# A planned attention-and-MLP kernel whose order planner gets other landing latencies for software loads, and an order searched with them

## The chip, the cores and the metric

The kernel runs on one core of one Trainium2 chip. Its engines are TensorE (PE in the profile, with its weight loads as PEld), VectorE (DVE), ScalarE (ACT), GpSimd (POOL) and SyncE (SP). The metric is the device time of one execution in microseconds, lower is better; it is given as the median of several runs. One execution is also recorded by the hardware profiler.

## The reference

Two stages follow each other. The first is causal attention in a window of 128 positions with ALiBi slopes, over 8 batches and 8 heads, 576 positions and a head dimension of 64. The second is a two-layer MLP with a squared ReLU over the 4608 tokens.

```python
scores = scale * q @ k.T                      # per batch and head, 576 x 576
mask = (rel >= 0) & (rel < 128)               # rel = query position - key position
scores = where(mask, scores - slope[h] * abs(rel), -1e9)
attn = exp(scores - max); attn /= sum(attn)
x = (attn @ v) laid out as 4608 tokens x 512
h = x @ w_in                                  # 512 x 2048
out = (relu(h) ** 2) @ w_out                  # 2048 x 512, float32
```

## The kernel before, in words

**Tiles.** The 576 positions of a batch are five blocks: four of 128 and one of 64. There are 40 blocks (m = 0 to 39), numbered in the order in which they are handled: first block 0 of every batch (m = 0 to 7, "diag": only the block's own keys), then the others, two batches at a time. The 4608 tokens are nine groups g of 512 tokens, each of four ranges of 128 tokens; a range is one block, or two half blocks. A block's path is: load of k, q and v (cast to bf16 by the load), transposes of k and q (`tp`, on PE for m below 8, by a DMA transpose issued on SP after that), scores (`s`, L520), exp (`e`, ACT), mask (`m`, DVE), product with v (`pv`, L587), reciprocal and norm (`r`, `n`, DVE), transpose of x into `xT` (`xp`, on PE for m below 8, a DMA transpose on SP after that, L617).

**MLP steps.** For groups 0, 1 and 2 the first product is done in small units: `u{g}.{r}.{e}` (L721) multiplies range r of the group (128 tokens in group 0, 256 in groups 1 and 2) with 4 or 2 column blocks of `w_in`, so that one unit always fills a PSUM bank of 512 columns. Later groups use `fc{g}.{fc}` (L739) on 512 tokens. Each is followed by a relu on ACT (L692) and a square on DVE (L683). The second product is `o{g}.{t}.{part}` (L766), a quarter of the contraction over 2048 for 128 tokens: four matmuls of 512 columns. The work list puts all first-product steps of group 0 first, and then alternates one first-product step of group g+1 with one output step of group g. Item i has key 4i.

**Weights.** `w_in` and `w_out` are loaded in four quarters each (i0 to i3 and o0 to o3, L357 and L360) by software loads issued on POOL, as are all blocks but k and q of block 0, which come by hardware queues of SP and ACT. In group 0 a unit of element e needs quarter ie of `w_in`. `FIRST` is the order in which POOL issues the blocks 0 to 7 and the eight quarters.

**The planner.** `Plan` does not run on the chip: it fixes, when the kernel is built, the order in which every engine gets its instructions. Each task has an engine or a choice of them, a duration, a key and what it depends on. `Plan.order` steps through time by its own model: among the tasks that an engine could start within `NEAR` ns of the earliest, it takes the one of lowest key. A transfer takes the DMA engines from `max(start + FIRST, dma_free)` for `dma` ns, and counts as landed `LAND` ns (or the task's own `lat`) after that:

```python
at = max(st + self.FIRST[e], self.dma_free)
self.dma_free = at + t.dma
t.end = self.dma_free + (self.LAND[e] if t.lat is None else t.lat)
```

At most eight transfers of each kind (software or hardware) are outstanding (`LANES`). What an engine gets is then executed in order: when the plan believes that a load lands earlier than it does, the instruction that needs it stands in the queue, and everything behind it on that engine waits too. Where the plan sees PE idle for over 200 ns in its first 30 us, `fill` puts small matmuls on zeros into the gap (L269), in number 0.7 of the gap divided by 56 ns. `ADJ` adds an amount to the key of single named tasks; it is the result of a search. Blocks from 8 on have the key of the first work item that needs them, less `LEAD`. `N_CUT` blocks have their `xT` copied in two halves, and the first `N_PVH` jobs take the PSUM banks of `pv` from ring "h" (two banks, shared with the units and transposes) instead of ring "a" (four banks, shared with the scores).

Of the kernel before, what the change touches and what calls it, by code (L numbers as in the profile page):

```python
# [9 lines left out]
BF16 = mybir.dt.bfloat16  # L10
# [2 lines left out]

FIRST = ["b0", "b1", "b2", "i0", "i1", "o0", "i2", "b3", "i3", "o1", "o2", "o3", "b4", "b5", "b6", "b7"]
DIAG = [[0], [1], [2], [3], [4, 5], [6, 7]]
N_HW = 1
N_PE = 8
N_CUT = 2  # L20
N_PVH = 1
N_WARM = 8
FILL = 0.7
LEAD = 1160
IOTA = 3
TP, XP = "h", "h"
UNITS = {0: 128, 1: 256, 2: 256}
CUT = 384
SIZE = {"kq": 4, "v": 9, "kqT": 7, "P": 3, "x": 3}
DUE = {m: 200.0 * m - 1e5 for m in range(40)}  # L30

ADJ = {
    "e1.1": 9000135.6, "e19.2": -177.01, "e19.3": -468.76, "e2.1": 100084.3, "m2.0": 690.7, "m6.1": 98674.82,
    "mask0.6": 99479.82, "n6.1": 98853.62, "o0.1.2": -273.16, "o0.2.1": 39, "o0.3.2": -120.75, "o1.1.0": -108.3,
    "o1.2.3": -99095.7, "o1.3.1": -36.0, "o1.3.2": -98248.6, "o1.3.3": -224.85, "o2.0.0": -99746.7, "o2.0.1": -614.83,
    "o2.0.2": -99764.0, "o2.0.3": -321.48, "o2.2.1": -99007.0, "o2.3.0": -99983.4, "o2.3.1": -875.31,
    "pv0.1": 99179.79, "pv17.0": -148.06, "r0.1": 582.3, "reluu0.0.1": -99432.0, "reluu0.2.2": -9000091.1,
    "reluu0.2.3": -99589.6, "reluu1.0.0": -99692.3, "reluu2.1.2": -52.84, "s13": 168.43, "s17": -99446.52,
    "s20": 342.83, "squ0.1.0": 48, "squ0.2.3": 99864.0, "u0.1.0": -79.4, "u0.1.1": -99420.7, "u0.2.1": -99696.3,
    "u0.2.3": -98883.7, "u1.0.1": -98012.9, "u1.1.3": -99531.7, "u1.1.5": 191.7, "u1.1.6": -410.31,  # L40
    "u2.0.4": -100055.4, "u2.0.5": -342.1, "u2.0.6": -100078.7, "u2.0.7": -331.83, "u2.1.1": 78.7, "u2.1.2": 63.7,
    "u2.1.3": -99113.3, "u2.1.4": -79.4, "u2.1.7": -303.48,
}


def FUSED(g, u):
    return False


class Task:  # L50
# [20 lines left out]
class Plan:  # L71
# [2 lines left out]
    LAT = {"PE": 210.0, "ACT": 60.0, "DVE": 80.0, "POOL": 200.0, "SP": 200.0, "ACTQ": 200.0}  # L74
    BEGIN = {"POOL": 840.0, "SP": 740.0, "ACTQ": 740.0, "ACT": 2550.0, "DVE": 860.0, "PE": 1190.0}
    FIRST = {"POOL": 1100.0, "SP": 1150.0, "ACTQ": 1150.0}
    LAND = {"POOL": 1200.0, "SP": 2200.0, "ACTQ": 900.0}
    TO_SP = 600.0
    LANES = 8
    NEAR = {"PE": 60, "ACT": 0, "DVE": 25}  # L80
    FILL_UNTIL = 30000.0

    def __init__(self, bufs):
# [108 lines left out]
def kernel(  # L192
    ctx: ExitStack, tc: tile.TileContext, q, k, v, moe_w_in, moe_w_out, out
):
    nc = tc.nc
# [78 lines left out]
    def act(n):  # L274
        return n * 0.95 + 115.0
# [4 lines left out]
    def dve_p(n, rate=1):  # L280
        return n / rate / 0.96 + 185.0
# [65 lines left out]
    t_zero = plan.add({"DVE": 1300.0}, -1e5 + 950, zero, name="zero", later=25000.0)  # L347


    t_win = [None] * 4  # L350
    t_wout = [None] * 4

    def load_w(which, n, key):
        def emit():
            w = d_ff // 4
            if which == "in":
                nc.gpsimd.dma_start(w_in_sb[:, :, n * w:(n + 1) * w],  # L357
                                    moe_w_in[:, n * w:(n + 1) * w].rearrange("(c p) f -> p c f", p=128))
            else:
                nc.gpsimd.dma_start(w_out_sb[:, 4 * n:4 * n + 4, :],  # L360
                                    moe_w_out[n * w:(n + 1) * w, :].rearrange("(c p) f -> p c f", p=128))
        t = plan.add({"POOL": 780.0}, key, emit, dma=2600.0, name=f"w_{which}{n}")
        (t_win if which == "in" else t_wout)[n] = t

    s_kq, s_v, t_kq, t_v = {}, {}, {}, {}

# [7 lines left out]
    def load_block(m, key):  # L374
# [10 lines left out]
        if split:  # L385
            stage = stages[m]
            t_l = []
            for i, src in enumerate((k, q)):
                for r, (eng, e) in enumerate((("SP", nc.sync), ("ACTQ", nc.scalar))):
                    def fetch(i=i, src=src, r=r, e=e):  # L390
                        e.dma_start(view(stage, i)[:, r], source(src, m, split)[:, :, r])
                    t_l.append(plan.add({eng: 740.0}, key + 0.1 * i, fetch, dma=330.0, lat=1000.0,
                                        name=f"l{'kq'[i]}{m}.{r}"))

            def cast_kq(i):
                w = slice(i * d_model, (i + 1) * d_model)
                copy((c_k, c_q)[i],
                     kq[s_kq[m].idx][:, w].rearrange("s (i r d) -> s r i d", i=4, d=D),
                     stage[:, w].rearrange("s (r i d) -> s r i d", r=2, d=D))
            engs = {"DVE": 480.0, "ACT": 600.0} if m else {"DVE": 480.0}  # L400
            c_q = None
            c_k = plan.add(engs, key, lambda: cast_kq(0), t_l[0:2], [s_kq[m]], name=f"ck{m}")
            c_q = plan.add(engs, key, lambda: cast_kq(1), t_l[2:4] + [c_k], name=f"cq{m}")
            t_kq[m] = [c_k, c_q]
        else:
            def fetch_kq():
                for i, src in enumerate((k, q)):
                    nc.gpsimd.dma_start(view(kq[s_kq[m].idx], i), source(src, m, split))  # L408
            t_kq[m] = [plan.add({"POOL": 1780.0}, key, fetch_kq, [], [s_kq[m]], dma=2 * ns,
                                name=f"lkq{m}", count=2)]  # L410
# [229 lines left out]


    def ups(g):
        if UP[g] == 512:
            return [("fc", g, u) for u in range(16)]
        return [("unit", g, r, e) for r in range(512 // UP[g]) for e in range(16 * UP[g] // 512)]

    UP = {g: UNITS.get(g, 512) for g in range(NG)}
    work_list = ups(0)
    for g in range(NG):
        up = ups(g + 1) if g + 1 < NG else []  # L650
# [1 line left out]
            work_list += up[u:u + 1] + [("o", g, u // 4, u % 4)]  # L652

    def span_of(item):
        w = UP[item[1]]
        lo = item[1] * 512 + (item[2] * w if w < 512 else 0)
        return lo, lo + w

    def blocks(lo, hi):
        return [at[x] for r in range(lo // 128, hi // 128) for x in ranges[r]]  # L660
# [10 lines left out]

    g_slots, g_sq, g_first, o_slots = {}, {}, {}, {}

    def relu_square(g, slot, last_mm, key, out_of, fused):
        def square(a, b=None):
            if g_slots[g].tile is None:
                g_slots[g].tile = work.tile([128, FCB, 512], BF16, tag="g", bufs=2, name="g")
            o = out_of(g_slots[g].tile)
            i = a if len(o.shape) == 2 else a.rearrange("p (f t) -> p f t", f=o.shape[1])
            if fused:  # L680
                nc.vector.scalar_tensor_tensor(o, i, 0.0, i, op0=ALU.max, op1=ALU.mult)
            else:
                nc.vector.tensor_tensor(o, i, i, op=ALU.mult)  # L683
        if fused:
            ts = plan.add({"DVE": dve_p(512)}, key, lambda: square(slot.tile), [last_mm] + g_sq[g][:1], [], [slot],
                          name=f"rs{g}")
        else:
            srt = Slot("rt")

            def relu():  # L690
                srt.tile = work.tile([128, 512], BF16, tag="rt", bufs=3, name="rt")
                nc.scalar.activation(srt.tile, slot.tile, AF.Relu, bias=0.0, scale=1.0)  # L692
            tr = plan.add({"ACT": act(512)}, key, relu, [last_mm], [srt], [slot], name=f"relu{last_mm.name}")
            ts = plan.add({"DVE": dve(512, 2)}, key, lambda: square(srt.tile), [tr] + g_sq[g][:1], [], [srt],
                          name=f"sq{last_mm.name}")
        g_sq[g].append(ts)
        return ts

    def group(g):
        if g not in g_slots:  # L700
# [1 line left out]
            return [g_slots[g]]  # L702
        return []

    sq_of = {}

    def unit(g, r, e, key):

        new = group(g)
        slot = Slot("h")  # L710
        w = UP[g]
        nf = 512 // w
        lo = g * 512 + r * w
        ms = blocks(lo, lo + w)

        def emit():
            fill(t_mm, bank_of(slot, "h"))
            for f in range(nf):
                fc = nf * e + f
                for cc in range(C):  # L720
                    nc.tensor.matmul(slot.tile[:, f * w:(f + 1) * w], w_in_sb[:, cc, fc * 128:(fc + 1) * 128],  # L721
                                     xT[:, cc, lo:lo + w], start=cc == 0, stop=cc == C - 1)
        t_mm = plan.add({"PE": 4 * nf * mm(w)}, key, emit,
                        [t_win[nf * e // 4], g_first.get(g)] + [x for m in ms for x in t_x[m]], [slot] + new,
                        name=f"u{g}.{r}.{e}")
        g_first.setdefault(g, t_mm)
        ts = relu_square(g, slot, t_mm, key,
                         lambda gt: gt[:, nf * e:nf * e + nf, r * w:(r + 1) * w], FUSED(g, e + r))
        for t in range(r * w // 128, (r + 1) * w // 128):
            sq_of.setdefault((g, t, nf * e // 4), []).append(ts)  # L730

    def fc_step(g, fc, key):
# [3 lines left out]
        def emit():  # L736
            bank(slot, "h")
            for cc in range(C):
                nc.tensor.matmul(slot.tile, w_in_sb[:, cc, fc * 128:(fc + 1) * 128],  # L739
                                 xT[:, cc, g * 512:(g + 1) * 512], start=cc == 0, stop=cc == C - 1)  # L740
        t = plan.add({"PE": 4 * mm(512)}, key, emit,
                     [t_win[fc // 4], g_first.get(g)] + [x for m in blocks(g * 512, g * 512 + 512) for x in t_x[m]],
                     [slot] + new, name=f"fc{g}.{fc}")
        g_first.setdefault(g, t)
        ts = relu_square(g, slot, t, key, lambda gt: gt[:, fc, :], FUSED(g, fc))
        for r in range(4):
            sq_of.setdefault((g, r, fc // 4), []).append(ts)

# [84 lines left out]
```

The softmax here doesn't subtract the row's maximum and nothing guards it: scores larger than these inputs give would overflow.

## Time and profile before

| What | Value |
|---|---|
| runs | 316.77 us, median of 3 (316.46 to 316.91) |
| profiled execution | 316.23 us, its span 314.4 us |
| mean granted TensorE clock | 0.994 |
| software loads (queue 0) | 18.10 MB |
| weight quarters, issue to landing | w_in 10.9 us, w_out 15.0 us (medians of 4) |
| block loads, issue to landing | 6.2 to 7.6 us (medians) |

The span runs from the first to the last instruction; the time has 1.8 us more around it. A digit of a slice row is the busy share of 1/40 of the span in tenths, and the row PEclk is the clock granted to TensorE. In a group's row, busy time and mean duration are followed by the idle time ahead of it and by what ended it. A matmul's duration includes its way through the array, so matmuls in a row overlap; how many start in a stretch says more than their mean duration.

### The profile page before, as it was taken

To read this page: it belongs to the slowest core of one execution; us is meant where nothing else is said; L and a number is where in the kernel's file an instruction comes from. 1 tells how busy PE (TensorE), PEld (TensorE's weight loads), DVE (VectorE), ACT (ScalarE), POOL (GpSimd) and SP (SyncE) were. 2 spreads that over 40 slices of the span, in tenths; PEclk is the share of its full clock that TensorE was granted. 3 is DMA by queue.
4 is the path that set the end of the run, shared out by engine and by line. 5 is a ranking of instruction groups with operands and counts; after the bars stand their busy time and mean duration, and the time that the engine had idled before them with its cause. 6 is when DMAs were issued, how large, how long until landed. Compare 5 with 4: busy or idle time off the path is not lost.

```text
span 314.4 us, 7113 instructions
## 1 busy us (share of the span) xinstructions
PE 306.3 (97%) x2794; PEld 176.0 (56%) x2794; DVE 174.1 (55%) x498; ACT 170.7 (54%) x331; POOL 105.5 (34%) x131
## 2 busy tenths in 40 slices
PE   8789999999999999999999999999999999999996
PEld 4679756776766755454554555545554444444443
DVE  3756467766566666776766666666666222222211
ACT  4646436657657625776576655576464443434400
POOL 8826598352622666320966301800000000000000
PEclk9979999999999999999999999999999999999999
DMA  9999999999999999994999999992221100010022
GB/s 134 181 190 206 171 184 163 160 153 171 187 138 138 162 189 167 181 143 95 127 196 170 180 107 122 191 161 83 52 63 23 67 35 34 34 35 33 33 93 76
DMA packets 165714, 39.54 MB, mean 126 GB/s; under 512 B 156336, under 2 KB 161200, under 8 KB 165680
## 3 DMA queue, kind: packets, MB, share of 16 engines
q0 software_dynamic: 114656, 18.10, 84.5%
q1 hardware_dynamic: 50592, 20.65, 34.9%
q8 instruction: 22, 0.36, 0.5%
q10 hardware_dynamic: 432, 0.33, 0.3%
q14 instruction: 12, 0.10, 0.1%
HBM read 36.70 MB, written 9.44 MB: 147 GB/s over the span
## 4 chain that ended last, share of the span: by engine, by line
PE 92%; DMA 5%; POOL 2%; issue 0%; ACT 0%; POOLq 0%
PE o L766 39%; PE h L739 27%; PE h L721 14%; PE pv L587 6%; PE s L520 5%; DMA w_in_sb<-in_moe_w_in_dram 3%; DMA xT<-x 2%; POOL kq L408 1%; POOL vf L413 1%; PE tp L464 1%; PE xp L629 0%; POOL w_in_sb L357 0%; POOL dist L304 0%; ACT osb L290 0%; POOLq L304 0%
## 5 line engine op out<-in xcount | busy, mean ns | idle before, releaser
L766 PE MATMUL o<-w_out_sb,g 128*128 128x512 bf16 (+2 forms) x592 | 142.4, 373 | 0.0
L692 ACT ACTIVATE rt<-h 128x512 bf16<-128x512 f32 x144 | 85.8, 609 | 91.4 <-PE h L739 63.3
L683 DVE TENSOR_TENSOR g<-rt 128x512 bf16<-128x512 bf16 x144 | 60.3, 422 | 66.8 <-ACT rt L692 66.0
L739 PE MATMUL h<-xT,w_in_sb 128*128 128x512 bf16 x384 | 96.1, 379 | 0.0
L766 PEld LDWEIGHTS <-g 128*128 128x128 bf16 x592 | 54.5, 98 | 56.5
L544 ACT ACTIVATE P<-s 128x512 bf16<-128x512 f32 (+1 forms) x136 | 67.2, 582 | 17.3 <-PE s L520 17.3
L739 PEld LDWEIGHTS <-w_in_sb 128*128 128x128 bf16 x384 | 34.6, 98 | 38.2
L552 DVE TENSOR_TENSOR P<-P,masks 128x512 bf16<-128x512 bf16 (+1 forms) x112 | 44.6, 405 | 14.7 <-ACT P L544 9.8
L721 PE MATMUL h<-xT,w_in_sb 128*128 128x128 bf16 (+1 forms) x512 | 47.9, 250 | 3.0 <-DMA w_in_sb<-in_moe_w_in_dram 2.3
L408 POOL DMA_DIRECT2D kq<-in_k_dram x39 | 33.4, 856 | 36.4 <-DMA kqT<-kq 26.9
L721 PEld LDWEIGHTS <-w_in_sb 128*128 128x128 bf16 x512 | 39.7, 100 | 8.7 <-DMA w_in_sb<-in_moe_w_in_dram 2.7
L413 POOL DMA_DIRECT2D vt<-in_v_dram x32 | 27.2, 855 | 46.2 <-PE pv L587 43.7
L408 POOL DMA_DIRECT2D kq<-in_q_dram x39 | 33.5, 860 | 8.3 <-DMA kq<-in_q_dram 2.4
L609 DVE TENSOR_TENSOR x<-pv,rec 128x256 bf16<-128x256 f32 (+1 forms) x80 | 33.8, 423 | 2.7
L587 PEld LDWEIGHTS <-P 128*128 128x128 bf16 (+1 forms) x576 | 25.6, 101 | 14.1 <-DVE P L559 1.7
L290 ACT ACTIVATE osb<-o 128x512 f32<-128x512 f32 (+1 forms) x24 | 14.2, 590 | 23.4 <-PE o L766 23.4
L605 DVE RECIPROCAL rec<-pv 128x4 f32<-128x4 f32 (+1 forms) x80 | 14.2, 178 | 22.7 <-PE pv L587 20.2
L587 PE MATMUL pv<-vt,P 128*128 128x65 bf16 (+1 forms) x448 | 24.0, 194 | 0.0
L288 DVE COPY osb<-o 128x512 f32<-128x512 f32 (+1 forms) x13 | 8.9, 681 | 15.1 <-PE o L766 14.6
L520 PEld LDWEIGHTS <-kqT 64*128 64x128 bf16 x448 | 12.4, 94 | 7.6 <-issue 7.2
L520 PE MATMUL s<-kqT 64*128 64x128 bf16 (+1 forms) x256 | 15.6, 210 | 0.0
L520 PE MATMUL s<-kqT,kqT 64*128 64x128 bf16 (+1 forms) x192 | 11.4, 210 | 0.0
(40 smaller groups left out, 96.3 us busy)
## 6 DMA issues: line engine op xcount, KB each, us to landing
out_dram<-osb SPq DMA_DIRECT2D x31, 256.0 KB, 5.1
kq<-in_k_dram POOLq DMA_DIRECT2D x31, 128.0 KB, 6.9
kq<-in_q_dram POOLq DMA_DIRECT2D x31, 128.0 KB, 7.6
vt<-in_v_dram POOLq DMA_DIRECT2D x24, 128.0 KB, 7.6
w_in_sb<-in_moe_w_in_dram POOLq DMA_DIRECT2D x4, 512.0 KB, 10.9
w_out_sb<-in_moe_w_out_dram POOLq DMA_DIRECT2D x4, 512.0 KB, 15.0
vf<-in_v_dram POOLq DMA_DIRECT2D x8, 128.0 KB, 6.2
out_dram<-osb SPq DMA_DIRECT2D x8, 128.0 KB, 2.4
```

Source lines behind the costliest of these rows:

```text
L408: nc.gpsimd.dma_start(view(kq[s_kq[m].idx], i), source(src, m, split))
L413: nc.gpsimd.dma_start(tile_of(s_v[m])[0:n, :, 0:D], source(v, m))
L520: nc.tensor.matmul(sS[2 * g2 + r].tile[:, jj * 256 + c0:jj * 256 + c0 + w], tile_of(s_kqT[mk])[rows, c, :], tile_of(s_kqT[mq])[rows, C + c ...
L544: nc.scalar.activation(flat(Pt[sP.idx]), sS[i].tile.rearrange("p (j t) -> p j t", j=2)[:, :, lo:hi], AF.Exp, bias=0.0, scale=scale)
L552: nc.vector.tensor_tensor(flat(Pt[sP.idx]), flat(Pt[sP.idx]), flat(masks), op=ALU.mult)
L587: nc.tensor.matmul(sv.tile[0:n, hi * (D + 1):(hi + 1) * (D + 1)], Pt[sP.idx][:, place(h)].rearrange("p t q -> p (t q)")[:, w], tile_of(s_v ...
L609: nc.vector.tensor_tensor(xt[sx.idx][0:n, hf * 256:(hf + 1) * 256].rearrange("p (h e) -> p h e", h=4), heads(sv)[0:n, :, 0:D], sr.tile[0:n ...
L683: nc.vector.tensor_tensor(o, i, i, op=ALU.mult)
L692: nc.scalar.activation(srt.tile, slot.tile, AF.Relu, bias=0.0, scale=1.0)
L721: nc.tensor.matmul(slot.tile[:, f * w:(f + 1) * w], w_in_sb[:, cc, fc * 128:(fc + 1) * 128], xT[:, cc, lo:lo + w], start=cc == 0, stop=cc ...
L739: nc.tensor.matmul(slot.tile, w_in_sb[:, cc, fc * 128:(fc + 1) * 128], xT[:, cc, g * 512:(g + 1) * 512], start=cc == 0, stop=cc == C - 1)
L766: nc.tensor.matmul(slot.tile[:, 0:hi - lo], gt[:, fc, t * 128:(t + 1) * 128], w_out_sb[:, fc, lo:hi], start=fc == 0, stop=fc == FCB - 1)
```

## The change

The latency from the end of a software transfer to its landing becomes 2400 ns for blocks (1200 before) and 2900 ns for weights. The two k loads of block 0 get 1650 ns and the two q loads 700 ns (1000 before). In `FIRST` block 3 moves ahead of the third quarter of `w_in`. `N_CUT`, `N_PVH`, `LEAD` and `NEAR` get other values, and `ADJ` is another table. The unit sizes are written as lists with the same sizes as before, the quarters of `w_in` as a list `PIECES` of four equal pieces, and a path for a fused relu and square that was never taken is removed.

```diff
-FIRST = ["b0", "b1", "b2", "i0", "i1", "o0", "i2", "b3", "i3", "o1", "o2", "o3", "b4", "b5", "b6", "b7"]
+FIRST = ["b0", "b1", "b2", "i0", "i1", "o0", "b3", "i2", "i3", "o1", "o2", "o3", "b4", "b5", "b6", "b7"]
...
-N_CUT = 2
-N_PVH = 1
+N_CUT = 1
+N_PVH = 0
...
-LEAD = 1160
+LEAD = 720
...
-UNITS = {0: 128, 1: 256, 2: 256}
+UNITS = {0: [(0, 128, 4), (128, 128, 4), (256, 128, 4), (384, 128, 4)], 1: [(0, 256, 2), (256, 256, 2)],
+         2: [(0, 256, 2), (256, 256, 2)]}
+PIECES = [4, 4, 4, 4]
...
 ADJ = {
...
-    "u2.1.3": -99113.3, "u2.1.4": -79.4, "u2.1.7": -303.48,
+    "e1.2": 99737.5, "e14.1": 197.91, "e16.2": -128.81, "e19.2": -8999803.95, "e2.3": -401.4, "e20.1": 2.03,
+    "e3.1": 99809.35, "e6.3": 99108.3, "fc3.1": -547.61, "fc3.2": -237.14, "fc3.3": -684.14, "fc3.5": -652.43,
+    "fc3.7": -100007.3, "fc3.8": -9000379.3, "m18.2": 165.47, "m18.3": -239.22, "n1.1": 100203.0, "n10.1": 495.17,
...
+    "u0.2.0": -8999828.5, "u0.2.1": -99868.0, "u1.1.0": 39, "u1.1.1": -99305.4, "u1.1.4": -99991.3,
...
 }
...
-    LAND = {"POOL": 1200.0, "SP": 2200.0, "ACTQ": 900.0}
+    LAND = {"POOL": 2400.0, "SP": 2200.0, "ACTQ": 900.0}
...
-    NEAR = {"PE": 60, "ACT": 0, "DVE": 25}
+    NEAR = {"PE": 25, "ACT": 60, "DVE": 25}
...
-        t = plan.add({"POOL": 780.0}, key, emit, dma=2600.0, name=f"w_{which}{n}")
+        t = plan.add({"POOL": 780.0}, key, emit, dma=650.0 * (hi - lo), lat=2900.0, name=f"w_{which}{n}")
...
-                    t_l.append(plan.add({eng: 740.0}, key + 0.1 * i, fetch, dma=330.0, lat=1000.0,
+                    t_l.append(plan.add({eng: 740.0}, key + 0.1 * i, fetch, dma=330.0, lat=700.0 if i else 1650.0,
...
-            tr = plan.add({"ACT": act(512)}, key, relu, [last_mm], [srt], [slot], name=f"relu{last_mm.name}")
+        tr = plan.add({"ACT": act(n)}, key, relu, [last_mm], [srt], [slot], name=f"relu{last_mm.name}")
...
-        ts = relu_square(g, slot, t_mm, key,
-                         lambda gt: gt[:, nf * e:nf * e + nf, r * w:(r + 1) * w], FUSED(g, e + r))
+        ts = relu_square(g, slot, t_mm, key, lambda gt: gt[:, nf * e:nf * e + nf, at_r:at_r + w], nf * w)
```

In every unit `nf * w` is 512, so relu and square keep their shapes.

## The prediction

> **What bounds the kernel now.** I read the page first. Its engine shares and its 40 slices say that TensorE is the bound, and that it is short of full at the two ends only.
>
> ```profile
> span 314.4 us, 7113 instructions
> PE 306.3 (97%) x2794; PEld 176.0 (56%) x2794; DVE 174.1 (55%) x498; ACT 170.7 (54%) x331; POOL 105.5 (34%) x131
> PE   8789999999999999999999999999999999999996
> PEclk9979999999999999999999999999999999999999
> ```
>
> The third digit of PEclk is a 7: the clock fell once, between 15.7 and 23.6 us. "Busy" hides that, so I cut this stretch out with the table by stage (columns: us, then busy us and instructions of PE, PEld, DVE, ACT, POOL, then granted clock, DMA share, GB/s).
>
> ```profile
> 14.00:17.56 3.56, 1.24 (x20) 1.01 (x18) 1.75 (x7) 0.98 (x2) 0.85 (x2) 0.95 1.24 207
> 17.56:20.80 3.24, 3.24 (x36) 3.24 (x37) 1.02 (x4) 0.60 (x1) 1.20 (x2) 0.53 1.26 203
> 20.80:25.69 4.89, 4.89 (x80) 4.42 (x78) 2.80 (x18) 3.98 (x12) 2.47 (x4) 1.00 1.84 182
> ```
>
> TensorE is idle for 2.3 of the first 3.56 us and then runs at 0.53 of its clock for 3.24 us (0.47 x 3.24 = 1.5 us lost). Together 3.8 us of TensorE time go here. The PE timeline names the waits.
>
> ```profile
> 14.99 1.07 PE L721 MATMUL h<-xT,w_in_sb 128*128 128x128 bf16 x16 [0.93 <-DMA w_in_sb<-in_moe_w_in_dram]
> 15.89 0.28 PE L629 MATMUL xp<-ident,x 128*128 128x128 bf16 x2
> 17.56 1.89 PE L721 MATMUL h<-xT,w_in_sb 128*128 128x128 bf16 x16 [1.40 <-DMA w_in_sb<-in_moe_w_in_dram]
> 19.25 0.64 PE L587 MATMUL pv<-vf,P 128*128 128x65 bf16 x8
> ```
>
> The first quarter of w_in (i0) lands at 14.99, the second (i1) at 17.56. An i1 unit stands in PE's in-order queue ahead of block 2's pv, whose last mask ended at 16.70 on DVE, and ahead of every further i0 unit. From 17.56 on TensorE never waits for more than 0.65 us until the tail. So the end moves only by what is saved near the start, unless a later supply runs out.
>
> **The change part by part.**
>
> *Landing constants.* I follow the planner's transfer clock by hand. The stage loads of block 0 and its v end at 4080, kq1 at 5820, v1 6690, kq2 8430, v2 9300, i0 11900, i1 14500, o0 17100 ns. With LAND 1200 it believes kq1 at 7.0, kq2 at 9.6, i0 at 13.1, i1 at 15.7, o0 at 18.3 us. With 2400 for blocks and 2900 for weights it believes 8.2, 10.8, 14.8, 17.4, 20.0. The trace: PE waits for q1 until 8.16, q2 until 10.77, i0 until 14.99, i1 until 17.56; POOL's last w_out issue waits for o0 until 20.34. The new beliefs are right to about 0.3 us, the old ones 1.1 to 2.0 early. A rule speaks against two constants: the Trainium skill, "DMA: Bandwidth & Descriptors", section "Anatomy of one DMA — SWDGE (gpsimd) path", gives a software load a fixed part of about 2.0 us that scales with nothing. With it i0 would be expected at 13.9 and the plan would still place things 1.1 us early. The landings leave 2.3 us for q2 (10.77 - 8.43) and 3.1 for i0 (14.99 - 11.90), so I take the change's values.
>
> *What that can fill.* Between 14.99 and 17.56 the work with i0 alone is the units of rows 0, 1 and 2 (0.89 us each, the chain's row "27.16 0.89 PE h L721 x16"), pv2 (two bursts of 0.24) and xp2 (0.22): 2.67 + 0.70 = 3.4 us for 2.57 us of time. Row 2 is the late one: s2 ran at 12.0, its exps end at 13.5, masks and norms are short on DVE, so x2 can be there near 16.7. ADJ's entry for "u0.2.0" (-8999828.5) asks for just that unit early. So this stretch can be full, and then no half clock follows. Waits that the planner now foresees also get fill matmuls (line 269), which the before lacks at 14 to 17.6 because it foresaw none.
>
> *b3 ahead of i2.* Three block loads of 0.87 us of issue each pass one weight issue on POOL and one transfer on the software queue. In the before i2 landed by 23.15 (POOL's wait ends there) and i3 by 28.24; b3's three transfers lie between and take 28.2 - 23.1 - 2.6 = 2.5 us. So i2 comes 2.5 us later, near 25.6; b3 comes 2.6 us earlier: k, q, v near 20.9, 21.7 and 22.5. i3 and everything behind it keep their places: POOL's eight outstanding loads only swap whom they wait for, and the order behind i3 is the same. SP and ACT issue nothing of this.
>
> *The sum at 25.6 us.* In the before, 7 units and 1 output step had begun and ended there (timeline to 25.69): 7 x 0.89 + 0.86 = 7.1 us, beside pv2 and xp2. In the changed order what exists before i2 is 6 units (rows 0 to 2 with i0 and i1), 3 output steps with o0 (20.3 us on), and b3's tp, s and pv: 5.34 + 2.58 + about 1.15 (tp 0.45, s 0.45, pv 0.25) = 9.1 us. It fits: i1 units from 17.6 to 20.3, output steps to 22.9, b3 between, then a hole of about 1.7 us until i2, unavoidable as nothing else has landed. Gain 9.1 - 7.1 = 2.0 us, and behind it both orders are full. Its ends: 3.4 us if i2 and b3 land as the planner believes (25.2) and the hole holds more of b3; 1.0 if the queue is blocked again by a landing that is 0.3 to 0.5 us late.
>
> *Clock at that hole.* A rule is to be weighed here. The row: the stretch 14.00 to 17.56 held 1.24 us of work, its longest gap was 1.40 us, and the half clock followed. The Trainium skill, "TensorE: Matmul & The Clock Gate", section "HAM oscillation — how this bites in real kernels", asks only that no idle gap exceed about 3.4 us; by it neither this drop nor one at the new hole should occur, and the 1.5 us would be no part of any sum. The row decides: a stretch 35% busy was enough. The new hole leaves its stretch about half busy, more with fills; the stretch 12.00 to 14.00 in the before was 74% busy and kept the clock. Cost between 0 and 1.5 us; I take 0, being nearer to the stretch that kept it once fills run.
>
> *N_CUT 1, N_PVH 0.* One xT copy for block 1 instead of two of 0.38 us on ACT: 0.2 us saved on an engine that waits for PE then; the whole x1 now waits for the second norm (DVE 0.42), hidden by i0's landing at 14.99. Block 0's pv takes "a" banks, which can hold back s1 by a norm (0.6 us) at 9.4 us; five microseconds of cover remain before i0. Both zero; with the cover gone 0.2 and 0.6.
>
> *LEAD 720, NEAR, ADJ.* The last group's blocks get due 960 - 720 = 240, the key of work item 60, which PE has passed by about 85 us; all other blocks stay at or near the front as before. So LEAD should move little by itself. The stall of 0.65 us at 80.52 (PE waits for a transposed block) is a misplaced wait: six output steps of group 1 were still undone. A new order may drop it or put another in its place: 0.65 either way, I take +0.3.
>
> Units keep their sizes, w_in its four pieces, relu and square their 512 columns (ACT 609, DVE 422 ns): zero, as the instructions are the same.
>
> Sum: 2.0 + 0.3 = 2.3 us off the profiled execution (316.23; span 314.4 and 1.8 around it), which is 0.5 under the median of the runs. Off the median: **316.77 - 2.3 = 314.5**.
>
> **The rivals.**
>
> *The gain is given back later.* Blocks come at DMA's pace, and being ahead uses up slack. From the chain I counted output steps: when group 1's first unit starts at 51.2 one step of group 0 is left; at 80.52 six steps of group 1; at 120.5, when group 3 starts, one step of group 2.
>
> ```profile
> 51.37 1.75 PE h L721 x16
> 74.45 6.03 DMA xT<-x
> 80.52 2.79 PE h L721 x24
> 117.42 1.73 PE o L766 x8
> 119.70 0.97 PE o L766 x4
> 120.67 1.73 PE h L739 x8
> ```
>
> Group 3 needs block 16's transpose, issued on SP at 111.81, plus the page's 5.7 us to landing: 117.5. At 117.5 four output steps (3.5 us) were left. So up to about 3.5 us of gain survives there. If half of that slack is not usable in queue order, 1 us survives: 315.8.
>
> *Half clock at the new hole.* 2.0 + 0.3 - 1.5 to 1.7 = 0.6 to 0.8 off: about 316.1. For it: 35% busy was enough. Against: fills.
>
> *Slower: block 16 comes a turn later.* The 32 transposes of x run from 63.7 to 242.0 us, one per 5.75 us. If the altered keys let another block's SP transpose pair go first, block 16 lands near 123.3 instead of 117.5. PE, 2.3 us ahead, has 3.5 - 2.3 = 1.2 us left at 117.5 and stands idle 4.6 us: net 2.3 us slower, 319.1. It decides from a delay of 3.5 us on (there the early gain is eaten up). Against it: SP's order follows block order, and PE waits in the before are small.
>
> *The change doesn't do what it says:* the other order is as good as the old and the landings only move a wait from i1 to i2: within 0.6 us of the before, 316.6.
>
> **How the numbers follow.** This kernel's measurement tells about 0.2% (0.63 us) from no change. The early hole filled, gain 1.2 to 3.4: 0.68. Given back later, gain 0.7 to 1.2: 0.09. Half clock at the hole: 0.10, of which 0.06 count as faster. No effect: 0.05. Slower: 0.08. So faster 0.83, same 0.09, slower 0.08. The range 313.3 to 316.4 runs from a gain of 3.4 to the half-clock case and leaves out the slow case and half of "no effect".
>
> **What would show it.** In the changed profile: three i0 units and pv2 before the first i1 unit; granted clock near 1 from 15 to 21 us; b3's tp at 21 to 22 instead of 25.7; a hole or line-269 fills just before 25.6; group 1's first unit about 2 us before 51.2 and group 3's about 2 us before 120.5; the tail (last 16 us) unchanged. I am wrong if the clock falls again near 25 to 28, or if PE idle appears at 51, 80 or 118.

## The result, and the profile after

The changed kernel takes 314.24 us (median of 4 runs, 313.98 to 314.68), the kernel before 316.76 (median of 4). The ratio is 0.9923 with a 95% interval of 0.9906 to 0.9940: 2.5 us, or 0.8%, faster. The profiled executions stand closer, 316.23 and 314.68 (spans 314.4 and 312.9): that of the kernel before is below all its other runs, that of the changed kernel is its slowest. What follows explains the 1.5 us between these two, and uses ratios for what is beyond them.

The changed kernel's page, and its table by stage for the stretches shown of the kernel before (us, then busy us and instructions of PE, PEld, DVE, ACT, POOL, then granted clock, DMA share, GB/s):

```profile
span 312.9 us, 7112 instructions
PE 302.9 (97%) x2777; PEld 175.3 (56%) x2820; DVE 171.1 (55%) x492; ACT 173.2 (55%) x336; POOL 105.6 (34%) x131
```

```profile
14.00:17.56 3.56, 2.43 (x42) 2.07 (x41) 1.96 (x9) 1.86 (x5) 0.80 (x2) 1.00 1.24 207
17.56:20.80 3.24, 2.67 (x38) 2.36 (x40) 2.71 (x9) 1.91 (x7) 1.04 (x2) 1.00 2.07 169
20.80:25.60 4.80, 4.80 (x71) 3.89 (x70) 2.52 (x17) 2.42 (x8) 3.09 (x4) 1.00 1.31 205
```

The clock stays at 1.00 (0.53 before in the second row), and PE has 2.43 us of work instead of 1.24 in the first. The matmul counts are not to be compared closely: records are missing here (2777 matmuls beside 2820 weight loads), so some of the "idle" of PE is none. The PE timeline shows what the order has become:

```profile
15.18 1.07 PE L718 MATMUL h<-xT,w_in_sb 128*128 128x128 bf16 x16 [0.94 <-DMA w_in_sb<-in_moe_w_in_dram]
16.20 0.41 PE L593 MATMUL pv<-vf,P 128*128 128x65 bf16 x8
16.61 0.39 PE L635 MATMUL xp<-ident,x 128*128 128x128 bf16 x4
17.76 1.96 PE L718 MATMUL h<-xT,w_in_sb 128*128 128x128 bf16 x32 [0.39 <-DMA w_in_sb<-in_moe_w_in_dram]
...
50.22 1.91 PE L718 MATMUL h<-xT,w_in_sb 128*128 128x256 bf16 x16
...
78.13 1.91 PE L718 MATMUL h<-xT,w_in_sb 128*128 128x256 bf16 x16
...
118.60 3.62 PE L735 MATMUL h<-xT,w_in_sb 128*128 128x512 bf16 x16
```

Block 2's pv stands ahead of the first i1 unit. The first unit of group 1 starts at 50.22, the first of group 2 at 78.13. In the kernel before they start at 51.20 and at 80.52, the second after a wait of 0.65 us:

```profile
51.20 1.91 PE L721 MATMUL h<-xT,w_in_sb 128*128 128x256 bf16 x16
80.52 2.79 PE L721 MATMUL h<-xT,w_in_sb 128*128 128x256 bf16 x24 [0.65 <-DMA xT<-x]
```

The waits of PE in the changed kernel (us in total, times, longest) hold no more than 0.4 us behind 25 us:

```profile
PE s L526 <- DMA kqT<-kq: 0.2, 1, 0.2
PE o L762 <- issue: 0.2, 1, 0.2
```

So the gain is 1.0 us by 50 us and 2.4 us at group 2's start, of which 1.5 are left at the end. Of the 2.4 us, 1.0 is the early part, 0.65 the wait that is gone, and the rest is work that is still to be done. The table by stage for the output steps alone (L766 before, L762 after; PE, then weight loads) counts them up to group 2's start, first before, then changed:

```profile
0.00:80.50 80.50, 25.72 (x104) 9.27 (x104) 0.98 1.80 169
```

```profile
0.00:78.10 78.10, 23.16 (x90) 8.95 (x100) 1.00 1.81 169
```

Four weight loads are one step: 26 steps before, 25 after, while units (384 weight loads), scores (128) and pv (112) are the same. One step is 0.86 us, and 2.39 - 0.86 = 1.53 us.

**Where the other wait went.** The timeline of SP, first of the kernel before, then of the changed one:

```profile
63.72 1.20 SPq L617 DMA_TRANSPOSE xT<-x  x1
73.12 1.23 SPq L450 DMA_TRANSPOSE kqT<-kq  x1
74.45 1.29 SPq L617 DMA_TRANSPOSE xT<-x  x1
```

```profile
67.52 2.51 SPq L623 DMA_TRANSPOSE xT<-x  x2
72.32 7.45 SPq L456 DMA_TRANSPOSE kqT<-kq  x3
```

Block 9's x is complete when its last norm ends at 70.06 us on DVE in the kernel before. Its transpose is issued only at 74.45, because block 12's kq transpose stands ahead of it in SP's in-order queue and waits for its load (SP's waits there: "SPq L450 <- DMA kq<-in_k_dram: 7.5, 1, 7.5"). The old plan starts that transpose at about 67.8 us (the edit of experiment 5 puts block 9 just ahead of it), 5 us before it could be issued. In the changed kernel x of blocks 8 and 9 go first, at 67.5, and block 12's transpose follows at 72.3. Group 2's first unit needs blocks 8 and 9.

### The profile page after: what moved, and what is told of

Its sections match the earlier page's. It is cut to its first block, busy times and chain, and to the rows that moved or that the text cites. A ratio compares the mean times of both kernels' runs of the same rounds, so it can differ in the third digit from the quotient of the medians.

```text
span 312.9 us, 7112 instructions
## 1 busy us (share of the span) xinstructions
PE 302.9 (97%) x2777; PEld 175.3 (56%) x2820; DVE 171.1 (55%) x492; ACT 173.2 (55%) x336; POOL 105.6 (34%) x131
## 4 chain that ended last, share of the span: by engine, by line
PE 78%; DMA 16%; POOL 3%; issue 1%; ACT 0%; POOLq 0%; SPq 0%
PE o L762 34%; PE h L735 27%; PE h L718 7%; PE pv L593 5%; PE s L526 5%; DMA w_out_sb<-in_moe_w_out_dram 5%; DMA kqT<-kq 3%; DMA vf<-in_v_dram 3%; DMA kq<-in_q_dram 3%; DMA w_in_sb<-in_moe_w_in_dram 2%; POOL kq L414 2%; POOL vf L419 1%; POOL vt L419 0%; POOL dist L305 0%; ACT osb L291 0%
## 5 line engine op out<-in xcount | busy, mean ns | idle before, releaser
L762 PE MATMUL o<-w_out_sb,g 128*128 128x512 bf16 (+2 forms) x565 | 138.4, 373 | 1.9 <-DMA w_out_sb<-in_moe_w_out_dram 0.3
L735 PE MATMUL h<-xT,w_in_sb 128*128 128x512 bf16 x368 | 95.1, 379 | 0.8
L762 PEld LDWEIGHTS <-g 128*128 128x128 bf16 x592 | 54.1, 98 | 56.0 <-issue 0.4
L718 PE MATMUL h<-xT,w_in_sb 128*128 128x128 bf16 (+1 forms) x512 | 46.7, 246 | 1.3 <-DMA w_in_sb<-in_moe_w_in_dram 1.3
L291 ACT ACTIVATE osb<-o 128x512 f32<-128x512 f32 (+1 forms) x23 | 13.6, 592 | 21.0 <-PE o L762 20.8
```

The lines of the kernel that those rows point to most:

```text
L762: nc.tensor.matmul(slot.tile[:, 0:hi - lo], gt[:, fc, t * 128:(t + 1) * 128], w_out_sb[:, fc, lo:hi], start=fc == 0, stop=fc == FCB - 1)
```

## The experiments

Kernel n below is the kernel of experiment n. Beside these kernels the runs of the kernel before lie between 315.6 and 319.8 us (median 316.8 to 316.9 in each of three sets), so each kernel is given as a ratio to it with its interval, beside what its profile shows. Moves of single instructions are made by changing the planned start of a task after `plan.order()` and sorting again.

**1. Fills at the two early waits of the kernel before.**

```diff
+            for _ in range({"u0.0.0": 12, "u0.1.1": 20}.get(t_mm.name, 0)):
+                nc.tensor.matmul(slot.tile[:, 0:128], warm[:, 0:128], warm[:, 0:128], start=True, stop=True)
```

> The kernel before with 12 matmuls on zeros put ahead of the first i0 unit and 20 ahead of the first i1 unit, into PE's waits of 0.93 and 1.40 us; no other instruction moves. If the half clock from 17.6 to 20.8 us is what the idle of that stretch costs, the clock stays at 1.00 and the time falls by its loss of 1.5 us: about 315.3. If the half clock has another cause (the rival), or if the gain of the change is idle time filled with useful work alone, the time stays within 0.3 us of the kernel before.

Measured: 0.9914 (0.9881 to 0.9947), about 2.7 us (2.1 us between the medians); clock 1.00, and a mean clock of 0.999 or 1.000 in all six executions. But its profiled execution is only 0.8 us shorter than that of the kernel before (span 313.6), and that 0.8 us is seen at group 2's start: 79.69 instead of 80.52, with a wait of 0.74 us for block 9. What PE gained early beyond that stood still there. The time agrees with the first theory, the profile doesn't show the path; the two are not reconciled. Block 12's kq transpose was issued at 72.45 there, 0.7 us earlier than in the kernel before; whether loads came earlier still in the other executions is not on record.

**2. Block 2's pv ahead of the first i1 unit in the kernel before** (`"u0.1.1": 17325.0`).

> The kernel before with one unit, u0.1.1 (the first that needs i1), moved behind the two pv bursts of block 2 in PE's order; all else as it was. If the wrong landing cost 0.5 us of useful work stuck behind the i1 wait and no more, the time falls by 0.5 us: 316.3. If the 0.5 us of work are also enough to keep the clock (busy share of the stretch up from 35% to 49%), it falls by 2.0: 314.8, with the clock at 1.00 from 17.6 to 20.8 us.

Measured: 1.0010 (0.9987 to 1.0032), no gain, although in the profiled execution the move did what it should: clock 1.00 from 17.6 to 20.8 us, group 1 begun at 49.81 instead of 51.20. Both expectations fall: of the 22 executions only 8 had a mean clock of 1.000, and those have a median of 316.35, not 314.8. The PE timeline says where 1.4 us went:

```profile
81.12 2.79 PE L721 MATMUL h<-xT,w_in_sb 128*128 128x256 bf16 x24 [2.65 <-DMA xT<-x]
```

Group 2 begins at 81.12 after a wait of 2.65 us; without it PE would have been there at 78.47. Block 12's kq transpose was issued at 73.12 and block 9's x at 74.44, as in the kernel before to 0.01 us.

**3. The changed kernel without the late fills** (`FILL_UNTIL = 14000.0`).

> The changed kernel without the fill matmuls planned later than 14 us (17 fewer, about 1 us of PE time, same order otherwise). If the fills hold the clock, it falls to half for some 3.3 us after 17.6 and the time rises by up to 1.5 us: 315.7. If useful work alone (about 53% of the stretch) holds it, the time stays at 314.2.

Measured: 0.9924 (0.9895 to 0.9954), as the changed kernel; clock 1.00 with PE busy for 2.40 of 3.56 us, and a mean clock of 1.000 in 10 of 11 executions. The fills behind 14 us are not needed.

**4. The landing constants alone, in the kernel before.**

```diff
-    LAND = {"POOL": 1200.0, "SP": 2200.0, "ACTQ": 900.0}
+    LAND = {"POOL": 2400.0, "SP": 2200.0, "ACTQ": 900.0}
...
-dma=2600.0, name=f"w_{which}{n}")
+dma=2600.0, lat=2900.0, name=f"w_{which}{n}")
...
-lat=1000.0,
+lat=700.0 if i else 1650.0,
```

> The kernel before with the new landing latencies alone (2400 ns for blocks, 2900 for weights, the two of block 0), and the old FIRST, ADJ, LEAD, NEAR, N_CUT and N_PVH. If right landings are the whole of the gain, 314.3. If the order must be searched anew with them (the old key table was made for other beliefs), the early gain of 1.5 to 2 us comes, and is given back behind 20 us by units and blocks in a worse order: 316 to 318.

Measured: 1.0081 (1.0048 to 1.0114), 2.6 us slower. PE waits 2.28 us for block 9's x, and runs the next 16 matmuls at a clock of 0.50 (80.10 to 83.00 us):

```profile
80.10 3.45 PE L721 MATMUL h<-xT,w_in_sb 128*128 128x256 bf16 x16 [2.28 <-DMA xT<-x]
```

The plan that results still has block 12's kq transpose ahead of block 9's x (issued at 72.99 and 74.32 us), so the constants alone don't cure that order. Right beliefs with a key table made for wrong ones are worse than both wrong.

**5. Block 9's x transpose ahead of block 12's kq transpose, in the kernel before** (`"x9": 67825.0`): two neighbours on SP change places, nothing else.

> The kernel before with block 9's x transpose issued on SP ahead of block 12's kq transpose instead of behind it; nothing else moves. In the kernel before, SP waits with block 12's transpose until 73.1 us for its k load, and block 9's x, whose norm ended at 70.1, is issued at 74.45. If this is what holds PE at 80.5 us (0.65 us), the wait goes and the time falls by 0.6 us. If x lands late for another reason (the queue behind it), nothing changes.

Measured: 0.9942 (0.9924 to 0.9960), 1.8 us faster, three times what was expected.

```profile
64.66 5.55 SPq L617 DMA_TRANSPOSE xT<-x  x2
73.45 1.23 SPq L450 DMA_TRANSPOSE kqT<-kq  x1
```

```profile
78.64 2.78 PE L721 MATMUL h<-xT,w_in_sb 128*128 128x256 bf16 x24
```

Group 2 begins at 78.64 without a wait, 1.9 us before 80.52. Not all of this is the wait of 0.65 us. In this execution the clock was 1.00 up to there, with the PE order of the kernel before and the same wait of 1.40 us for i1, but i0 and i1 landed 0.7 us earlier and PE did not wait for i0:

```profile
14.32 1.07 PE L721 MATMUL h<-xT,w_in_sb 128*128 128x128 bf16 x16
16.90 1.07 PE L721 MATMUL h<-xT,w_in_sb 128*128 128x128 bf16 x16 [1.40 <-DMA w_in_sb<-in_moe_w_in_dram]
```

Group 1 began at 49.35, 1.85 us before the 51.20 of the kernel before; a wait of 0.71 us for a kq transpose at 57.26 came in, and that of 0.65 us for block 9 went. So the half clock of the earlier profile is not in every execution, and what the exchange did was to let an early gain through that would have stood still at the wait for block 9. The clocks of all executions, below, agree with it.

**6. Both moves, 2 and 5.**

> The kernel before with both moves: block 2's pv ahead of the first i1 unit, and block 9's x transpose ahead of block 12's kq transpose. With the first move alone PE came to the wait for block 9 earlier and stood there for 2.65 us. If the wait gave the early gain back, both together fall by 2.0 to 2.7 us, to the time of the changed kernel (314.2). If the early move brings nothing of its own, they fall by no more than the 0.6 us of the second move.

Measured: 0.9944 (0.9921 to 0.9967), as move 5 alone; in the profile group 2 begins at 78.38 and the span is 312.3. It is between the two expectations: the pv move adds 0.3 us in the profiles and nothing that the times could show.

**7. The converse in the changed kernel: block 12's kq transpose ahead of block 9's x** (`"kqT12": 69457.0`).

> The changed kernel with block 12's kq transpose moved ahead of block 9's x transpose on SP, as in the kernel before. Block 9's x would be issued after 72.3 plus 1.3 us instead of near 69, land 6 us later near 79.6, and PE, which begins group 2 at 78.1, would wait for it: 1.4 us slower, 315.6. If SP's order there doesn't matter, the time stays.

Measured: 1.0009 (0.9989 to 1.0030): this one exchange takes all of the gain back.

```profile
71.45 1.24 SPq L456 DMA_TRANSPOSE kqT<-kq  x1
72.78 1.41 SPq L623 DMA_TRANSPOSE xT<-x  x1
```

```profile
79.65 1.91 PE L718 MATMUL h<-xT,w_in_sb 128*128 128x256 bf16 x16 [1.12 <-ACT P L550]
```

Group 2 begins at 79.65 after a wait that the profile puts down to ACT. Block 9's x is a likelier cause: issued at 72.78, and with the 4.6 to 6.7 us to landing of the x transposes of that stretch, it landed by 79.5. The span is 314.4. By this profile, at full clock, the exchange costs 1.5 us, by the ratios more (0.9923 to 1.0009, 2.7 us).

**8. The changed kernel with the old FIRST**, i2 ahead of b3.

> The changed kernel with the old FIRST alone (third quarter of w_in ahead of block 3), the rest as changed. If block 3 ahead of i2 is worth the 2 us that the prediction gave to the early part, 316; if the early part lives from the clock and the order behind the i1 wait, within 0.5 us of 314.2, unless the key table, made for the other order, misplaces later blocks: then up to 1.7 us slower with waits behind 50 us.

Measured: 1.0047 (1.0029 to 1.0066), 4 us slower than the changed kernel. Group 1 begins at 51.54 with 16 output steps done, in the changed kernel at 50.22 with 15 (64 and 60 weight loads of the output steps): with the step taken off, 0.5 us later. The greater part comes after that. The plan that results has block 12 ahead of blocks 8 and 9 on SP again, and another wait of 1.10 us for an x at 94.89:

```profile
62.42 10.76 SPq L456 DMA_TRANSPOSE kqT<-kq  x2
73.27 2.98 SPq L623 DMA_TRANSPOSE xT<-x  x2
```

```profile
80.03 1.91 PE L718 MATMUL h<-xT,w_in_sb 128*128 128x256 bf16 x16 [1.40 <-DMA xT<-x]
```

**9. The changed kernel with the old landing constants.**

> The changed kernel with the old landing latencies alone (1200 ns for blocks and weights, 1000 for block 0's k and q). The planner then puts block 12's kq transpose ahead of the x transposes of blocks 8 and 9 on SP again, and an i1 unit ahead of block 2's pv. If SP's order there is what the landing constants are worth, PE waits for block 9's x near 80 us and the time is that of the kernel before or worse: 316.5 to 318. If the new key table alone is worth the gain, 314.2.

Measured: 1.0010 (0.9992 to 1.0029). SP issues block 12's transpose, then blocks 8 and 9 at 72.97, as expected; but the expected wait near 80 us is not in the profile. Group 2 begins at 79.51 with one output step more done than in the changed kernel (104 weight loads instead of 100), so a step filled the time. A wait of 1.33 us stands at 120.06, ahead of group 3; the profile names no cause for it. The key table alone is worth nothing.

**10. The changed kernel with LEAD 1160.**

> The changed kernel with LEAD 1160 instead of 720. The prediction said that LEAD moves little by itself: within 0.4 us of 314.2. If the later attention steps are better spread with 720, it is slower by 1 us or more.

Measured: 0.9996 (0.9968 to 1.0024), a loss of the whole gain by the middle of the interval (316.44 in the six executions with a mean clock of 1.000). SP has blocks 8 and 9 in time (67.06), but PE's order puts a unit of group 2's second half, which needs block 11, in the seventh place (six units, 432 weight loads, were done by 90.6 us), and block 11's x was issued at 83.22:

```profile
90.67 1.03 PE L718 MATMUL h<-xT,w_in_sb 128*128 128x256 bf16 x8 [1.64 <-DMA xT<-x]
```

In the changed kernel all eight units of the first half come before 93.2.

**11. Three moves in the kernel before:** 2 and 5, and unit u0.1.0 with its relu and square ahead of the first i1 unit.

> The kernel before with three moves: block 9's x transpose ahead of block 12's kq transpose on SP, and in PE's order block 2's pv and then unit u0.1.0 (which needs i0 only, with its relu and square) ahead of the first i1 unit. If, with the wait at 80 us gone, early work counts in full, it is one unit, 0.9 us, below the two moves alone (ratio 0.9944): about 314.1 on the scale of 316.8. If another wait takes the gain, it stays there.

Measured: 0.9909 (0.9884 to 0.9934); group 2 begins at 78.33, span 312.6. Three exchanges in the old order are as good as the change. The intervals of this one and of kernel 6 overlap, and in the profiles group 2 begins only 0.05 us earlier, so the 0.9 us of the unit is not shown. What differs is the clock: 0.999 or 1.000 in all six executions here, 0.995 in four of the seven of kernel 6.

**12. The changed kernel with u0.1.0 early** (with block 1's second norm, transposes and copy).

> The changed kernel with block 1's second norm, its x transposes, their copy and the unit u0.1.0 moved ahead of the first i1 unit. The changed kernel idles or fills 1.7 us between 14.0 and 17.6 us; one unit of 0.89 us fits. If nothing later is short, 313.4. If the next supply (i2 near 25.6, or blocks 4 and 5) ends the gain, it stays at 314.2.

Measured: 0.9912 (0.9883 to 0.9941), no different from the changed kernel. No version here is clearly better than it.

**The starts of group 2 together.** From group 2's first unit to the end of the span the profiles need 233.9 us (before, 1, 6), 234.0 (2, 5), 234.3 (11) in the old order, and 234.8 or 234.9 (changed, 3, 7, 12) in the new one, where one more step is left. Ahead of that point the starts differ by 3 us, from 78.13 to 81.12. In these profiles the span is that start plus a constant. (Kernels 4, 8, 9 and 10 have orders of their own behind it and are left out.)

**The clock of the single executions.** Every execution has its mean clock on record. In the profile of the kernel before, a mean of 0.994 comes of one stretch at a clock of 0.50, from 17.2 to 20.6 us. The medians, by mean clock (number of executions):

| Kernel | 1.000 | 0.994 or 0.995 |
|---|---|---|
| before, three sets | 316.67 (32) | 316.85 (70) |
| 5, exchange on SP | 314.34 (7) | 315.65 (6) |
| 6, exchange and pv | 314.15 (2) | 315.62 (4) |
| 2, pv alone | 316.35 (8) | 318.32 (14) |
| 7, converse in the changed kernel | 316.23 (4) | 317.13 (7) |

In the kernel before a stretch of half clock hardly shows in the time (0.2 us). With block 9's wait gone it costs 1.3 us: in kernel 5 the slowest of the first group (314.73) is below the fastest of the second (315.35). So kernel 5's 1.8 us is a mixture, 2.3 us at full clock and 1.2 us with half clock, and at full clock kernel 5 is as fast as the changed kernel (314.22, three of its four executions). That kernel, together with kernel 3, ran at 1.000 in 13 of 15 executions, the kernel before in 32 of 118. By these rows the gain of the change has two parts: block 9's place on SP, and an early stretch full enough to hold the clock, which counts once block 9 is in time. The groups are executions as they fell; no edit set their clock. Kernels 2 and 7, which wait for block 9, lose 0.9 to 2.0 us at the lower mean; where their half clock lies is not on record, but kernel 4's profile has one right behind this wait. Kernel 1 doesn't fit: with the wait still there it is 1.9 us below the kernel before at full clock.

## Why the prediction was right or wrong

The time was forecast as 314.5 and is 314.24. The sum came out, its terms less so, and that is in part luck: between the two profiles 1.5 us of the 2.3 us came, of an early term half as large as forecast and a wait twice as large.

- **Landing beliefs and pv2 behind i1: right in what they move.** pv2 no longer stands behind the i1 wait (pv2 at 16.20, the first i1 unit at 17.76), and the clock is up. By itself the move of pv2 is worth nothing (kernel 2), and the constants by themselves cost 2.6 us (kernel 4).
- **The fill of the early stretch: mis-sized.** I expected three i0 units ahead of i1 and a hole before i2, with 2.0 us gained by 25.6. There is one unit, since block 1's second norm was put behind block 2's masks and x1 came late; and there is no hole, since the other i0 units were left for it. The gain at group 1's start is 1.0, with 15 output steps done in both kernels.
- **The stall at 80.52: the term that failed.** I called its 0.65 us "a misplaced wait" worth 0.3. It was the floor under the early part. In kernel 2 PE comes to it 1.4 us earlier and waits 2.65 us, because block 12's kq transpose is issued when its load lands (72.45 to 73.12 us in kernels 1, 2 and the one before) and block 9 follows it. Exchanging the two gives 1.8 us in the old order and takes the whole gain in the new one. I credited the gain to the first 26 us; in kernel 2 that part was given back at the wait, and in kernels 5 and 6 the clock's 1.3 to 1.5 us count in the time. Kernel 1, which gains without the exchange, stays open.
- **The first rival** ("the gain is given back later") named this place and asked for the slack in output steps. The count was right (six steps left), but in-order PE did not use them: the unit that waited stood ahead of the steps.
- **The slower rival** was a transpose of x behind another block's on SP. It is the mechanism of this case, with the other sign: the kernel before had it, for block 9, and the change removed it. My argument against it, that SP's order follows block order, was wrong for the kernel before: block 12's kq transpose stands ahead of block 9's x there.
- **LEAD: wrong.** "Should move little by itself" took no account of ADJ's entries of some hundreds (-482.59 for u2.1.2): with 1160 the plan has that unit of group 2's second half in the seventh place, with 720 in the ninth. Undone alone, LEAD costs the gain.
- **FIRST: right to count, wrong in what for.** The swap is worth 0.5 us by group 1's start (kernel 8), not 2.0; beyond that it is needed because the order was searched with it.
- **Clock at the new hole:** not tested by this change, as no hole came.

## What to carry to other kernels

In a queue that executes in order, an instruction placed too early because its input was believed to land sooner costs those behind it, and the costly one may stand on another queue than the stall: here a transpose on SP 60 us behind the loads on which the constants were fitted. Before crediting a gain near the start, look for the next start that hangs on a transfer and not on the engine, and ask what an earlier arrival would do there. For this planner, corrected constants and an order searched with them belong together: each alone gave nothing or a loss. They are not the only way: three exchanges in the old order gave as much (kernel 11).

## What was not expected of the hardware

- In the profile of the kernel before, the 3.56 us up to the landing of i1 held 1.24 us of PE work and no gap over 1.40 us, and the clock in the 3.24 us behind was 0.53. In kernel 5's profile, with the same PE order and the same gap of 1.40 us, the 3.56 us up to that landing (13.34 to 16.90) held 1.99 us of work, as PE did not wait for i0, and the clock stayed at 1.00.
- The same wait can be followed by either clock: 0.50 behind 2.28 us in kernel 4's profile, 1.00 behind 2.65 us in kernel 2's.
- Block 12's loads did not come earlier when PE was earlier: its transpose, which waits for them, was issued between 71.45 and 73.45 us in the kernel before, the changed one and kernels 1, 2, 5 and 7, while PE's start of group 1 lay between 51.20 and 49.35; the earliest start of group 1 (kernel 5) goes with the latest issue.
